# Moving one row tile's normalisation to GpSimd, and reordering the first norm, in a fused transformer block

## The chip, the cores and the metric

The kernel runs on one core of one Trainium2 chip. The metric is the device time of one execution in microseconds (us); lower is better.

Engine names: PE is TensorE (matmuls; PEld is its weight load, which overlaps it), DVE is VectorE, ACT is ScalarE, POOL is GpSimd, SP issues most of the DMA loads. The granted clock is the share of PE's full clock that a run's record shows (1.0 is full).

## The reference, cut to what matters

```python
mod = (_silu(c) @ w_mod).reshape(c.shape[0], 6, 1, -1)
sa, ca, ga, sb, cb, gb = ...                  # six rows of 1024: shift, scale, gate; twice
h = _layernorm(x, axis=-1) * (1 + ca) + sa    # x: 2048 x 1024, bf16
x = x + ga * _A_ref(h, A_wqkv, A_wo)          # linear attention; begins with h @ wqkv
h = _layernorm(x, axis=-1) * (1 + cb) + sb
x = x + gb * _B_ref(h, ...)                   # gated feed-forward, F = 3584
```

Only the start matters here. The first 512 rows of `x` (row tiles 0 to 3, each 128 x 1024) must be normalised, transposed and scaled before the first real matmul (q, the first third of `wqkv`) can run. The scale `ca` and shift `sa` are themselves products of 1 MB pieces of `w_mod` with one vector, done on PE as one-column matmuls.

## The kernel before: the parts in question

Every operation goes through a helper that derives the semaphore waits from the memory it touches, so the order of the calls is each engine's program order. The loads, on one DMA queue, in this order:

```python
for st in range(4):
    P.dma("x0_%d" % st, XRES[:, st, :], xv[:, st, :])      # 4 row tiles, 256 KB each
ca_load(0)        # scale columns 0-511, 1 MB, contiguous runs of 1024 bytes
wq_load(0, 2)     # query weights, rows 0-1 of 8 (each "row" is 128 x 1024)
ca_load(1)        # scale columns 512-1023
wq_load(2, 2); wq_load(4, 2)
sa_load(1)        # shift columns 512-1023
wq_load(6); wq_load(7)
sa_load(0)        # shift columns 0-511
```

The first norm, cut. `s0_`, `s1_`, `s3_` are the two `bn_stats` and the `bn_aggr` of tiles 0, 1 and 3 on VectorE; ScalarE sums tile 2 (`act_stats(2)`). `ln1_rstd1` adds epsilon on VectorE and takes the reciprocal root on GpSimd. `ln1_xn` normalises on VectorE, `ln1_xn_act(1)` on ScalarE:

```python
def ln1_xn(st):
    P.dve("tensor_scalar", out=XRES[:, st, :], in0=XRES[:, st, :],
          scalar1=MV[:, st, 0:1], scalar2=RSTD[:, st:st + 1], op0=ALU.subtract, op1=ALU.mult)

warm(13, bank=3)                       # matmuls on a constant, to keep PE's clock up
s0_[0](); s0_[1](); s1_[0](); s0_[2](); ln1_rstd1(0)
s1_[1](); s1_[2](); ln1_rstd1(1)
ln1_xn(0); tile_transposes(0); warm(5, bank=3)
s3_[0](); ln1_xn_act(1); tile_transposes(1)
m2[1](); m2[0](); neg_rstd(2)          # mean, variance, reciprocal root of tile 2
s3_[1](); s3_[2](); ln1_rstd1(3)
ln1_xn(2); ln1_xn(3)
mod_sc(WCA, 8, range(2)); fin_ca(0, 2) # scale columns 0-255: 16 one-column matmuls
tile_transposes(2, 3)
h0_first(0, "dve"); h0_first(1, "dve") # scaled, transposed tiles: q's operands
```

`q_phase_chunk0` then runs 4 q matmuls, the 16 one-column matmuls of scale columns 256-511, 10 more q matmuls, and so on; shift columns 512-1023 and 0-511 come in near the end of q.

The same `tensor_scalar` runs on GpSimd in one other place, on 128x512 pieces ahead of the feed-forward:

```python
P.pool("tensor_scalar", out=H2T[:, dt, :], in0=H2T[:, dt, :], scalar1=MODCOL[:, 2, dt:dt + 1],
       scalar2=MODCOL[:, 3, dt:dt + 1], op0=ALU.mult, op1=ALU.add)
```

## Time and profile before

| | before |
|---|---|
| median of 3 runs (lowest, highest) | 831.13 us (830.97, 832.21) |
| span of the profiled run | 829.3 us |
| PE busy | 823.3 us, 99% |
| first q matmul | 12.29 us |

The head of the page of the kernel before, with the busy time of each engine:

```profile
span 829.3 us, 10017 instructions
PE 823.3 (99%) x4083; PEld 378.8 (46%) x4083; DVE 312.9 (38%) x666; ACT 196.3 (24%) x335; POOL 40.5 (5%) x58
```

The end of the first part of the chain of waits (start, length, what), followed back from the last instruction:

```profile
9.78 0.79 POOL rstd L176
10.57 0.03 issue
10.60 0.56 DVE xres L176
11.16 0.05 issue
11.20 1.01 PE ps L176 x15
12.21 0.08 issue
12.29 814.80 PE ps L176 x4016
```

From 12.29 us on the chain is PE alone. Whatever delays the first q matmul, or makes PE wait after it, goes to the end of the program one to one. Ahead of it lies a chain over GpSimd (reciprocal root), VectorE (normalising tile 3) and PE (transposes).

PE's timeline of before around that point (start, busy time, instruction; in brackets the idle time before it and what ended it):

```profile
9.42 0.62 PE L176 MATMUL ps<-ident,xres 128*128 128x128 bf16 x8 [0.49 <-ACT xres L176]
9.87 0.54 PE L176 MATMUL ps<-siluc,wca 128*128 128x1 bf16 x16
...
11.20 1.01 PE L176 MATMUL ps<-ident,xres 128*128 128x128 bf16 x15 [0.71 <-DVE xres L176]
12.29 1.02 PE L176 MATMUL ps<-ht,wqk 128*128 128x512 bf16 x4
13.15 0.54 PE L176 MATMUL ps<-siluc,wca 128*128 128x1 bf16 x16
13.56 2.32 PE L176 MATMUL ps<-ht,wqk 128*128 128x512 bf16 x10
```

PE idles for short pieces before 12.29, then runs through, and the second block of 16 one-column matmuls (13.15) takes its time inside the solid stretch. GpSimd does four reciprocal roots in this time and is otherwise idle; the first two are those of tiles 0 and 1:

```profile
5.84 0.57 POOL L176 TENSOR_TENSOR rstd<-ve,neghalf 128x1 f32<-128x1 f32 x1 [4.44 <-DVE ve L176]
6.80 0.80 POOL L176 TENSOR_TENSOR rstd<-ve,neghalf 128x1 f32<-128x1 f32 x1 [0.39 <-DVE ve L176]
```

The view of one tile (minimum, median and maximum duration in ns, first and last start in us) gives GpSimd's existing `tensor_scalar`:

```profile
L176 POOL TENSOR_SCALAR h2t<-h2t,modcol x32: 762/768/1180, 230.9 to 649.4; 128x512 bf16<-128x512 bf16 x32
```

### The profile page before, as it was taken

Reading aid. Unit: us, or ns where it says so; the run is one execution under the profiler, and the core shown is the slowest. Engines: PE = TensorE matmul, PEld = TensorE weight load, DVE = VectorE, ACT = ScalarE, POOL = GpSimd, SP = SyncE. Lnnn points to the kernel's source line nnn. Section 1 sums busy time; section 2 is a strip of 40 time slices with the busy share of each in tenths; the row PEclk is TensorE's granted clock in tenths of the full one; section 3 lists DMA queues with packets and bytes.
Section 4 is the critical chain, followed back from the end, with each engine's and each line's share of the span. In section 5 each row is a group of like instructions: output and inputs, shape, how many; then the busy total and the mean of one; then the engine's idle time right before and its main releaser. Section 6 shows DMA issues by size and latency. Waiting matters only on the chain.

```text
span 829.3 us, 10017 instructions
## 1 busy us (share of the span) xinstructions
PE 823.3 (99%) x4083; PEld 378.8 (46%) x4083; DVE 312.9 (38%) x666; ACT 196.3 (24%) x335; POOL 40.5 (5%) x58
## 2 busy tenths in 40 slices
PE   8999999999999999999999999999999999999998
PEld 4544444454444444444444444444444444444444
DVE  5797986756955521121221111122111211221111
ACT  3658641323232111111111111111110111111011
POOL 1010000000130000030000003000000300000000
DMA  9969655938297986700455571045557004553000
GB/s 320 284 152 229 150 162 172 197 107 304 57 256 226 262 256 184 194 25 13 123 152 153 152 188 34 13 124 154 152 153 193 27 13 124 151 154 91 0 26 26
DMA packets 199246, 119.29 MB, mean 144 GB/s; under 512 B 57880, under 2 KB 182944, under 8 KB 199200
## 3 DMA queue, kind: packets, MB, share of 16 engines
q1 hardware_dynamic: 199184, 118.65, 53.0%
q8 instruction: 32, 0.52, 0.3%
q14 instruction: 14, 0.11, 0.0%
q10 hardware_dynamic: 16, 0.00, 0.0%
HBM read 100.67 MB, written 4.33 MB: 127 GB/s over the span
## 4 chain that ended last, share of the span: by engine, by line
PE 98%; DMA 1%; DVE 0%; ACT 0%; SPq 0%; POOL 0%; issue 0%
PE ps L176 98%; DMA xres<-in_A_x_dram 1%; ACT ht L176 0%; DVE xres L176 0%; SPq L176 0%; POOL rstd L176 0%; DVE stats L176 0%; DVE mv L176 0%; DVE ve L176 0%
## 5 line engine op out<-in xcount | busy, mean ns | idle before, releaser
L176 PE MATMUL ps<-h2t,gug 128*128 128x512 bf16 x896 | 211.7, 379 | 0.0
L176 PE MATMUL ps<-h2t,guu 128*128 128x512 bf16 x896 | 211.7, 379 | 0.0
L176 DVE TENSOR_TENSOR at<-sg,ps 128x512 bf16<-128x512 bf16 x112 | 77.0, 687 | 282.8 <-PE ps L176 281.2
L176 ACT ACTIVATE sg<-ps 128x512 bf16<-128x512 f32 x112 | 66.9, 597 | 309.7 <-PE ps L176 309.7
L176 PEld LDWEIGHTS ps<-h2t,guu 128*128 128x128 bf16 x896 | 87.7, 98 | 105.7
L176 PEld LDWEIGHTS ps<-h2t,gug 128*128 128x128 bf16 x896 | 87.6, 98 | 105.5
L176 PE MATMUL ps<-wd_a,at 128*128 128x512 bf16 (+1 forms) x512 | 112.4, 377 | 0.0
L176 PE MATMUL ps<-ht,wqk 128*128 128x512 bf16 x512 | 111.8, 379 | 0.1
L176 PE MATMUL ps<-wd_b,at 128*128 128x512 bf16 (+1 forms) x384 | 85.0, 377 | 0.0
L176 PEld LDWEIGHTS ps<-wd_a,at 128*128 128x128 bf16 x512 | 50.1, 98 | 59.7
L176 DVE TENSOR_TENSOR ut<-att,gb_b 128x512 bf16<-128x512 bf16 (+1 forms) x32 | 14.1, 441 | 167.0 <-ACT att L176 167.0
L176 PEld LDWEIGHTS ps<-ht,wqk 128*128 128x128 bf16 x512 | 49.4, 98 | 58.7 <-issue 0.2
L176 ACT ACTIVATE att<-ps 128x512 bf16<-128x512 f32 (+1 forms) x32 | 17.4, 591 | 182.1 <-PE ps L176 182.1
L176 PEld LDWEIGHTS ps<-wd_b,at 128*128 128x128 bf16 x384 | 37.6, 98 | 44.7
L176 PE MATMUL ps<-pk,xres 128*128 128x512 bf16 x256 | 56.5, 379 | 0.0
L176 PE MATMUL ps<-mw,pqt 128*128 128x512 bf16 x256 | 56.3, 379 | 0.0
L176 POOL TENSOR_SCALAR h2t<-h2t,modcol 128x512 bf16<-128x512 bf16 x32 | 26.3, 836 | 383.4 <-DMA h2t<-xn 383.4
L176 ACT ACTIVATE e<-ps 128x512 bf16<-128x512 f32 x56 | 33.1, 603 | 31.8 <-PE ps L176 21.3
L176 PEld LDWEIGHTS ps<-mw,pqt 128*128 128x128 bf16 x256 | 24.8, 98 | 30.2 <-DVE xres L176 0.4
L176 PEld LDWEIGHTS ps<-pk,xres 128*128 128x128 bf16 x256 | 24.8, 98 | 30.0 <-issue 0.4
L176 ACT ACTIVATE junk<-xres 128x1024 bf16<-128x1024 bf16 x24 | 25.4, 1058 | 35.1 <-DVE xres L176 34.9
L176 DVE SCALAR_TENSOR_TENSOR xres<-ps,xres 128x512 bf16<-128x512 f32 x32 | 21.4, 688 | 12.3 <-PE ps L176 11.5
(106 smaller groups left out, 345.1 us busy)
## 6 DMA issues: line engine op xcount, KB each, us to landing
gug<-in_B_w_gate_dram SPq DMA_DIRECT2D x56, 512.0 KB, 3.9
guu<-in_B_w_up_dram SPq DMA_DIRECT2D x56, 512.0 KB, 5.2
xres<-in_A_x_dram SPq DMA_DIRECT2D x20, 256.0 KB, 8.0
rb<-recip_den SPq DMA_DIRECT2D x8, 512.0 KB, 11.5
stgx<-in_w_mod_dram SPq DMA_DIRECT2D x2, 2048.0 KB, 7.8
wd_a<-in_B_w_down_dram SPq DMA_DIRECT2D x4, 1024.0 KB, 8.0
out_dram<-xres SPq DMA_DIRECT2D x31, 128.0 KB, 1.7
xres<-in_A_x_dram SPq DMA_DIRECT2D x3, 1024.0 KB, 14.2
```

The source lines that it names most:

```text
L176: return getattr(e, method)(**kw)
```

## The change

The intent: GpSimd, idle here, takes over tile 0, so that VectorE ends its sums earlier; scale columns 0-255 come in a load of their own and so earlier; and the matmuls of scale columns 256-511 move from the q phase into the time in which PE waits for q's first operand. The diff, cut:

```diff
-        ca_load(0)
+        ca_load(0, 256)
+        ca_load(256, 512)
         wq_load(0, 2)
-        ca_load(1)
+        ca_load(512, 1024)
...
+        def act_var(st): ...            # the variance of tile 2 in one step; one copy less
+        def xn_sums(st): ...            # ln1_xn with the mean read from ScalarE's sums
+        def xn_pool(st):
+            P.pool("tensor_scalar", out=XRES[:, st, :], in0=XRES[:, st, :],
+                   scalar1=MV[:, st, 0:1], scalar2=RSTD[:, st:st + 1], op0=ALU.subtract, op1=ALU.mult)
...
         s0_[0]()
         s0_[1]()
-        s1_[0]()
         s0_[2]()
         ln1_rstd1(0)
+        s1_[0]()
         s1_[1]()
         s1_[2]()
+        xn_pool(0)
         ln1_rstd1(1)
-        ln1_xn(0)
+        s3_[0]()
         tile_transposes(0)
-        warm(5, bank=3)
-        s3_[0]()
+        warm(3, bank=3)
+        mod_sc(WCA, 8, range(2))
+        s3_[1]()
         ln1_xn_act(1)
-        tile_transposes(1)
...
+        act_var(2)
         s3_[2]()
         ln1_rstd1(3)
-        ln1_xn(2)
+        xn_sums(2)
+        fin_ca(0, 2)
+        warm(1, bank=3)
+        tile_transposes(2)
+        tile_transposes(1)
         ln1_xn(3)
-        mod_sc(WCA, 8, range(2))
-        fin_ca(0, 2)
-        tile_transposes(2, 3)
+        tile_transposes(3)
+        mod_sc(WCA, 8, range(2, 4))
...
-            for nt in range(4):         # q phase
-                q_part(nt, qb[nt], (0,))
-            mod_sc(WCA, 8, range(2, 4))
```

Cut from this diff: the q matmuls on operand rows 0 and 1 are also grouped anew (both rows of the first four output groups, then of the other three), and `act_stats(2)` moves behind the call of `warm(13)`.

More of the change, by code (lines that the diff above doesn't have):

```diff
@@ L399, in bass_adaLN_cond__linear_attn_block__swiglu_ffn__prompt_kernel, with ca_load @@
             P.dma("x0_%d" % st, XRES[:, st, :], xv[:, st, :])
-        def ca_load(p):
-            P.dma("wca%d" % p, WCA[:, :, 512 * p:512 * p + 512], wmv[:, :, D + 512 * p:D + 512 * p + 512])
+        def ca_load(c0, c1):
+            P.dma("wca%d" % c0, WCA[:, :, c0:c1], wmv[:, :, D + c0:D + c1])
         def sa_load(p):
@@ L594, in neg_rstd, with act_var, xn_sums @@
             P.pool("tensor_tensor", out=RSTD[:, st:st + 1], in0=VE[:, st:st + 1], in1=NEGHALF[:, 0:1], op=ALU.pow)
-        act_stats(2)
         s0_, s1_, s3_ = ln1_stats_ops(0), ln1_stats_ops(1), ln1_stats_ops(3)
-        m2 = act_mv_ops(2)
+        def act_var(st):
+            P.dve("scalar_tensor_tensor", out=MV[:, st, 1:2], in0=SUMX[:, st:st + 1], scalar=SUMX[:, st:st + 1],
+                  in1=SUMSQ[:, st:st + 1], op0=ALU.mult, op1=ALU.subtract)
+            neg_rstd(st)
+        def xn_sums(st):
+            P.dve("tensor_scalar", out=XRES[:, st, :], in0=XRES[:, st, :],
+                  scalar1=SUMX[:, st:st + 1], scalar2=RSTD[:, st:st + 1], op0=ALU.subtract, op1=ALU.mult)
+        def xn_pool(st):
+            P.pool("tensor_scalar", out=XRES[:, st, :], in0=XRES[:, st, :],
+                   scalar1=MV[:, st, 0:1], scalar2=RSTD[:, st:st + 1], op0=ALU.subtract, op1=ALU.mult)
         def tile_transposes(*js):
@@ L607, in bass_adaLN_cond__linear_attn_block__swiglu_ffn__prompt_kernel @@
         warm(13, bank=3)
+        act_stats(2)
         s0_[0]()
         s0_[1]()
-        s1_[0]()
         s0_[2]()
         ln1_rstd1(0)
+        s1_[0]()
         s1_[1]()
         s1_[2]()
+        xn_pool(0)
         ln1_rstd1(1)
-        ln1_xn(0)
+        s3_[0]()
         tile_transposes(0)
-        warm(5, bank=3)
-        s3_[0]()
+        warm(3, bank=3)
+        mod_sc(WCA, 8, range(2))
+        s3_[1]()
         ln1_xn_act(1)
-        tile_transposes(1)
-        warm(0, bank=3)
-        m2[1]()
-        m2[0]()
-        neg_rstd(2)
-        s3_[1]()
+        act_var(2)
         s3_[2]()
         ln1_rstd1(3)
-        ln1_xn(2)
+        xn_sums(2)
[3 more added lines that the diff above has]
+        tile_transposes(1)
         ln1_xn(3)
-        mod_sc(WCA, 8, range(2))
-        fin_ca(0, 2)
-        tile_transposes(2, 3)
+        tile_transposes(3)
+        mod_sc(WCA, 8, range(2, 4))
         h0_first(0, "dve")
@@ L740, in q_phase_chunk0 @@
                 h0_first(dt, "dve")
-            for nts, dts in (((4, 5), (0,)), (range(6), (1,)), ((6,), (0, 1))):
+            for nts, dts in ((range(4), (0,)), (range(4), (1,)), ((4, 5, 6), (0, 1))):
                 for nt in nts:
```

## The prediction

> **What bounds the kernel now.** PE: the page gives it 823.3 us busy of a span of 829.3. The chain of waits holds one PE piece of 814.8 us that starts at 12.29 us (first q matmul) and never waits again. Before it lies the first norm, up to normalising tile 3 (until 11.15) and transposes (until 12.21). The change can gain only (a) an earlier q start and (b) scale matmuls moved out of the solid stretch into the idle time ahead of it.
>
> **What it removes, adds and moves (timeline of before).**
> - Normalising tile 0 leaves VectorE (0.54 us) for GpSimd. There 128x512 took 0.76 us; I estimate 1.5 us for 128x1024. Tile 1's reciprocal root on GpSimd then ends near 8.2, not 7.6 us; ScalarE has tile 2's sums until 8.23 anyway: tile 1 ready near 9.8, not 9.4.
> - VectorE finishes tile 3's statistics before tile 2's sums arrive and drops a copy (0.15 us). I estimate tile 2 ready at 10.15, tile 3 at 10.9 (before: 10.16 and 11.15).
> - Only 8 transposes, not 16, stay behind tile 3; then 16 scale matmuls (0.42 us of issue, before at 13.15 to 13.56) run while VectorE fills the first q operand. I estimate q to start at 12.0 to 12.1. Gain on PE alone: 0.6 us.
> - The 1 MB load of scale columns 0-511 becomes two of 0.5 MB; contiguous runs fall from 1024 to 512 bytes. In the trace 1024-byte packets took 47 to 52 ns, at 350 to 375 GB/s in the first 30 us; 512-byte ones (gate and up weights) 29 to 34 ns, at 290 to 330 GB/s. For 1 MB that is an estimated 0.45 to 0.65 us more. The Trainium skill, "DMA: Bandwidth & Descriptors", section "Why small descriptors are slow (HBM only)", names a fixed cost per packet; these times agree in direction.
>
> **How much lies on the critical path.** The DMA queue is full from 2 to 32 us, so a delay at its head reaches every later load. Landing against first use by PE: shift columns 512-1023 land at 20.79, used 21.05; shift columns 0-511 land at 25.16, used 25.38. Slack: 0.26 and 0.22 us. (Query weights: over 1 us.) A PE 0.6 us earlier catches up with these loads, and they come 0.45 to 0.65 us later. I expect shift columns 512-1023 at 21.2 to 21.45, PE waiting there 0.6 to 1.0 us, and the second shift load just in time. Net: the gain is lost and PE is 0.2 to 0.4 us later from 26 us on. Solid PE carries this to the end.
>
> **Prediction: 831.4 us**, range 830.5 to 832.3. Faster by over 2%: 0.01; within 2%: 0.98; slower by over 2%: 0.01.
>
> **What the profile would show.** Right: first q matmul at 11.9 to 12.3 us; a new PE wait for the shift columns near 20.5 to 21.4 us; 512-byte packets before 12 us at 28 to 34 ns; shift loads landing 0.3 to 0.7 us later; everything after 32 us unchanged in length. Wrong: no PE wait near 21 us and the span 0.5 us shorter (512-byte packets cost nothing here); or q starting after 13 us (GpSimd's normalisation takes longer than estimated).
>
> **What would make it wrong.** GpSimd taking over 2.5 us for tile 0, blocked by VectorE: the Trainium skill, "SBUF — State Buffer", section "SBUF: two separate sides", calls their shared port pair an exclusive lock; no run here shows it yet. Run-to-run spread (before: 830.97 to 832.21) exceeds the effect.

## The result, and the profile after

| | before | after |
|---|---|---|
| median of 6 runs (lowest, highest) | 831.17 us (830.83, 832.21) | 833.47 us (833.03, 833.79) |
| ratio of after to before | | 1.0026, 95% interval 1.0013 to 1.0039 |
| first q weight load | 12.26 us | 14.94 us |

Ratios here are the mean time of one kernel's fast runs over that of the other's in the same rounds, so they are not quite the ratio of the medians. At 2% the change is "same", as forecast. But it is slower by about 2.2 us, and 833.47 lies outside the stated range of 830.5 to 832.3.

GpSimd's timeline of the changed kernel:

```profile
5.35 0.56 POOL L176 TENSOR_TENSOR rstd<-ve,neghalf 128x1 f32<-128x1 f32 x1 [3.94 <-DVE ve L176]
6.01 3.79 POOL L176 TENSOR_SCALAR xres<-xres,mv,rstd 128x1024 bf16<-128x1024 bf16 x1
9.77 0.58 POOL L176 TENSOR_TENSOR rstd<-ve,neghalf 128x1 f32<-128x1 f32 x1
10.99 1.17 POOL L176 TENSOR_TENSOR rstd<-ve,neghalf 128x1 f32<-128x1 f32 x2 [0.64 <-DVE ve L176]
```

The instruction predicted at 1.5 us took 3.79. The reciprocal root of tile 1 has to queue behind it and ends at 10.35 us, not at 7.60 as before. VectorE takes its instructions in the order of the program here: the aggregation of tile 3's sums, which were complete at 8.33 us, came only at 10.83. So it stands still until that root is there, and with it the roots and normalisations of tiles 2 and 3:

```profile
7.04 1.29 DVE L176 BATCH_NORM_STATS2 stats<-xres 128x6 f32<-128x512 bf16 x2 [0.22 <-DMA xres<-in_A_x_dram]
10.38 0.21 DVE L176 TENSOR_SCALAR nmr<-mv,rstd 128x1 f32<-128x1 f32 x1 [2.06 <-POOL rstd L176]
10.83 0.20 DVE L176 BATCH_NORM_AGGREGATE mv<-stats 128x2 f32<-128x12 f32 x1
11.57 0.55 DVE L176 TENSOR_SCALAR xres<-xres,sumx,rstd 128x1024 bf16<-128x1024 bf16 x1 [0.36 <-POOL rstd L176]
12.52 0.54 DVE L176 TENSOR_SCALAR xres<-xres,mv,rstd 128x1024 bf16<-128x1024 bf16 x1
```

PE's timeline of the changed kernel:

```profile
9.86 0.86 PE L176 MATMUL ps<-ident,xres 128*128 128x128 bf16 x8 [2.28 <-POOL xres L176]
10.52 1.49 PE L176 MATMUL ps<-e,ident 128*128 128x512 bf16 x3
11.79 0.61 PE L176 MATMUL ps<-siluc,wca 128*128 128x1 bf16 x16
12.27 0.59 PE L176 MATMUL ps<-e,ident 128*128 128x512 bf16 x1
12.65 1.91 PE L176 MATMUL ps<-ident,xres 128*128 128x128 bf16 x24
14.40 0.54 PE L176 MATMUL ps<-siluc,wca 128*128 128x1 bf16 x16
```

PE waits 2.28 us for GpSimd's tile 0, and the second block of one-column matmuls now runs ahead of q, as intended. The chain of waits goes from GpSimd's tile 0 straight to PE, since the transposes of tile 0 stand first in PE's order:

```profile
6.01 3.80 POOL xres L176
9.81 0.05 issue
9.86 5.08 PE ps L176 x68
14.94 0.25 issue
```

So in this profile the result of the slow instruction is itself what PE waits for; the late roots lie beside the chain. From 9.86 us on PE has work without a wait up to q. One thing more is off: three warm-up matmuls took 1.49 us, where before five took 1.24. The view by stretches shows why (its first two columns are the stretch and its length, then the busy time of each engine, and the granted PE clock third from the end):

```profile
6.67:10.08 3.41, 1.13 (x8) 0.42 (x7) 1.43 (x3) 1.89 (x4) 3.41 (x2) 1.00 1.13 326
10.08:13.50 3.42, 3.42 (x36) 2.32 (x34) 1.93 (x8) 1.24 (x1) 1.43 (x3) 0.50 1.08 362
13.50:16.90 3.40, 3.15 (x42) 2.26 (x42) 2.42 (x6) 2.28 (x2) 0.00 (x0) 1.00 1.06 375
```

After a stretch in which PE worked 1.13 of 3.41 us, PE was granted half its clock for the next 3.41 us. The Trainium skill, "TensorE: Matmul & The Clock Gate", section "What's actually happening", describes it: a free-running window of 3413 ns, and half clock after an idle one. This trace agrees with the 3.41 us, though this window was 33% busy and not fully idle. Of the six timed runs four show it (granted clock 0.998 in the mean); these took 833.41 to 833.79 us, the two at full clock 833.03 and 833.27.

The account of the profiled run: the first q weight load is 2.68 us later (14.94 minus 12.26). (Weight loads are compared because one q matmul near the start is missing from the changed kernel's trace: 13 matmuls stand against 14 weight loads.) The weight load 3,800 from the end, which is past the shift work in both, is 2.28 us later (30.55 minus 28.27). The difference, 0.40 us, is about the 0.42 us of the moved block of one-column matmuls. So that part of the plan worked. The span grew by 2.4 us.

### The profile page after: what moved, and what is told of

Its sections match the earlier page's. It is cut to its first block, busy times and chain, and to the rows that moved or that the text cites. A ratio compares the mean times of both kernels' runs of the same rounds, so it can differ in the third digit from the quotient of the medians.

```text
span 831.7 us, 9937 instructions
## 1 busy us (share of the span) xinstructions
PE 820.3 (99%) x4004; PEld 379.9 (46%) x4082; DVE 312.2 (38%) x664; ACT 196.4 (24%) x335; POOL 44.2 (5%) x59
## 4 chain that ended last, share of the span: by engine, by line
PE 96%; DVE 2%; issue 1%; POOL 1%; DMA 0%; ACT 0%; DVEq 0%; ACTq 0%; POOLq 0%
PE ps L176 96%; DVE acc L176 1%; POOL xres L176 0%; DMA xres<-in_A_x_dram 0%; DVE pkt L176 0%; DVE stats L176 0%; DVE e L176 0%; DVE pqt L176 0%; DVE ht L176 0%; ACT e L176 0%; POOL rstd L176 0%; DVE xres L176 0%; DVE mv L176 0%; DVE modcol L176 0%; DVE ve L176 0%
```

## The experiments

All outputs are right. "Before" was run again in the same rounds each time.

### Why 3.79 us: three theories

*Operation*: GpSimd is slow at subtract-then-multiply. *Contention*: VectorE holds it up; VectorE's last sum ended at 8.33 us, and GpSimd ended 1.47 us later, at 9.80: just what a start at 8.33 and the estimated 1.5 us would give. *Size*: 1024 columns are slow.

**e0_probe**: the kernel before, with a ladder of GpSimd instructions on unused memory where GpSimd is idle, each form twice.

```diff
+ for _ in range(2):
+     probe(1024, ALU.mult, ALU.add, ml, ad)
+     probe(512, ALU.subtract, ALU.mult, me, rs)
+     probe(1024, ALU.subtract, ALU.mult, me, rs)
+     probe(512, ALU.mult, ALU.add, ml, ad)
+     ...  # 256 columns; in place; add-multiply; multiply-add with rs, me; multiply-subtract
```

> The kernel before, with a ladder of GpSimd tensor_scalar instructions on unused memory in the first chunk's down projection, where GpSimd is idle; each form twice: multiply-add and subtract-multiply at 256, 512 and 1024 columns, in place and not, plus add-multiply and multiply-subtract at 1024. Theory operation: multiply-add 1024 takes about 1.5 us and subtract-multiply 1024 about 3.8, 512 about 1.9. Theory size: both forms take 3.8 at 1024 and 0.76 at 512. Theory contention: both forms take 1.5 at 1024 where VectorE is quiet. The time of the kernel stays at 831.2 us, since GpSimd is idle there.

The time was 830.98 us (one run). GpSimd's timeline of this run; `mean,rstd` is subtract-multiply and `modcol` multiply-add, except the line at 375.89 (add-multiply) and the one at 378.48 (multiply-subtract):

```profile
361.36 1.20 POOL L176 TENSOR_SCALAR prb<-junk,modcol 128x1024 bf16<-128x1024 bf16 x1
362.66 2.08 POOL L176 TENSOR_SCALAR prb<-junk,mean,rstd 128x512 bf16<-128x512 bf16 x1
364.84 3.78 POOL L176 TENSOR_SCALAR prb<-junk,mean,rstd 128x1024 bf16<-128x1024 bf16 x1
370.00 1.26 POOL L176 TENSOR_SCALAR prb<-junk,mean,rstd 128x256 bf16<-128x256 bf16 x1
375.24 0.55 POOL L176 TENSOR_SCALAR prb<-junk,modcol 128x256 bf16<-128x256 bf16 x1
375.89 1.19 POOL L176 TENSOR_SCALAR prb<-junk,mean,rstd 128x1024 bf16<-128x1024 bf16 x1
378.48 3.79 POOL L176 TENSOR_SCALAR prb<-junk,rstd,mean 128x1024 bf16<-128x1024 bf16 x1
391.01 0.77 POOL L176 TENSOR_SCALAR prb<-junk,modcol 128x512 bf16<-128x512 bf16 x1
```

It is the operation, and within the pair it is the subtraction. Why GpSimd takes longer for it, no run here shows. Add-multiply and multiply-add take 1.19 to 1.20 us at 1024 columns; subtract-multiply and multiply-subtract take 3.78 and 3.79. From 512 to 1024 columns the slow form adds 1.70 us (3.3 ns a column), the fast one 0.43 us (0.84 ns). In place or not made no difference in the first pass (3.78 and 3.78); in the second the one in place took 3.96 us, beside VectorE `tensor_tensor` instructions. The expectation was off in one number: multiply-add at 1024 took 1.2 us, not the 1.5 that doubling gives. The Trainium skill, "GPSIMD Engine Reference", section 3.1, has 769 ns measured for 512 elements in its best case, which matches the 0.77 here; it says nothing of the subtraction. Contention exists too, but elsewhere: in the first pass multiply-add at 512 columns took 1.18 us, while VectorE ran `tensor_tensor` instructions with two SBUF inputs beside it.

**e3_quiet**: the changed kernel with VectorE kept silent while GpSimd works. Slower on purpose.

```diff
-        s1_[0]()
-        s1_[1]()
-        s1_[2]()
         xn_pool(0)
+        P.dve("tensor_copy", out=MODTMP[:, 15:16], in_=XRES[:, 0, 0:1])   # waits for GpSimd
+        s1_[0]()
+        s1_[1]()
+        s1_[2]()
```

> VectorE is kept silent while GpSimd normalises tile 0: a one-column copy on VectorE waits for GpSimd's result before tiles 1 and 3 are summed. Slower on purpose. Theory contention: GpSimd takes about 1.5 us (from 6.0 to 7.5 us). Theories operation and size: it takes 3.7 to 3.8 us as before, from 6.0 to 9.8 us.

VectorE and GpSimd in this run (836.28 us, one run):

```profile
6.21 3.78 POOL L176 TENSOR_SCALAR xres<-xres,mv,rstd 128x1024 bf16<-128x1024 bf16 x1
...
10.03 0.16 DVE L176 COPY modtmp<-xres 128x1 bf16<-128x1 bf16 x1 [4.64 <-POOL xres L176]
```

VectorE was idle for 4.64 us, over the whole of GpSimd's instruction, and it still took 3.78 us. Contention falls; the 9.80 us was a coincidence. This also agrees with the Trainium skill, "SBUF — State Buffer", section "Who interferes with whom", which says that a VectorE instruction with at most one SBUF input outside the two-port modes does not contend with GpSimd. `bn_stats` has one input here; whether it runs in a two-port mode, no run shows, but with it beside GpSimd the instruction took 3.79 us, and without it 3.78.

**e2_muladd**: the changed kernel with the same arithmetic on GpSimd in the fast form; the column minus-mean times rstd is made by VectorE in 0.16 us.

```diff
+        def xn_pool_ma(st):
+            P.dve("tensor_scalar", out=NMR[:, st:st + 1], in0=MV[:, st, 0:1], scalar1=RSTD[:, st:st + 1],
+                  scalar2=-1.0, op0=ALU.mult, op1=ALU.mult)
+            P.pool("tensor_scalar", out=XRES[:, st, :], in0=XRES[:, st, :],
+                   scalar1=RSTD[:, st:st + 1], scalar2=NMR[:, st:st + 1], op0=ALU.mult, op1=ALU.add)
-        xn_pool(0)
+        xn_pool_ma(0)
```

> GpSimd still normalises tile 0, but as multiply then add (x times rstd plus minus-mean-times-rstd) instead of subtract then multiply; VectorE makes the extra column. Theory operation: GpSimd is slow at this pair of operations, so it takes about 1.5 us (twice the 0.76 us of its 128x512 multiply-add), tile 0 is ready near 8.2 us instead of 9.8 and the time falls by 1 us or more. Theory contention (GpSimd is held up while VectorE works on its sums) and theory size (1024 columns are slow): it still takes 3 to 4 us, and the time stays at 833.5 us or above.

GpSimd's timeline of this run:

```profile
6.88 1.19 POOL L176 TENSOR_SCALAR xres<-xres,rstd,nmr 128x1024 bf16<-128x1024 bf16 x1 [0.98 <-DVE ve L176]
8.04 0.56 POOL L176 TENSOR_TENSOR rstd<-ve,neghalf 128x1 f32<-128x1 f32 x1
```

1.19 us instead of 3.79. The first q weight load went from 14.94 to 12.34 us. The median is 831.02 us against 830.87 of before in the same rounds, ratio 0.9999 (0.9985 to 1.0012). Changing the form of one instruction (and adding the column for it) takes the whole loss away.

### The other parts of the change

**e1_dve0**: tile 0 back on VectorE, the rest as changed (`xn_pool(0)` becomes `ln1_xn(0)`).

> Undoes one part of the change: tile 0 is normalised by VectorE again, at the same place in the order; loads and everything else as changed. If GpSimd's 3.79 us on tile 0 is what cost the time, q starts near 12.1 us (changed kernel: 14.9). Then two theories part. If that was the only loss, PE is 0.4 to 0.6 us ahead of the kernel before and the time is about 830.6 us. If the later landing of the loads also matters (in the changed kernel shift columns 512-1023 landed at 22.06 us instead of 20.79), PE now waits for them near 20.4 us for 0.7 to 1.6 us and the time is 831.5 to 832.2 us. If GpSimd was not the cause, the time stays at 833.5 us.

The median is 831.58 us (830.63 to 831.92) against 830.87; ratio 1.0002 (0.9989 to 1.0014). The first q weight load was at 12.52 us (I had expected 12.1). PE's weight loads show one new wait in the q phase, on query weights and not on the shift columns:

```profile
16.64 4.43 PEld L176 LDWEIGHTS ps<-ht,wqk 128*128 128x128 bf16 x22 [0.22 <-DMA wqk<-in_A_wqkv_dram]
```

The wait of 0.7 to 1.6 us for the shift columns that the second theory expected did not come. The wait shown costs PE 0.27 us: from the start of the 32 one-column matmuls to the next q matmul it is 1.07 us here (15.57 to 16.64) and 0.80 in the kernel before (15.71 to 16.51).

**e11_pool_only**: the kernel before, with tile 0 on GpSimd by subtract and multiply, and nothing else (`ln1_xn(0)` becomes the same instruction on GpSimd ahead of `ln1_rstd1(1)`).

> The kernel before with one part of the change alone: GpSimd normalises tile 0 by subtract and multiply, nothing else moves. Theory: the instruction takes 3.8 us, tile 1's reciprocal root behind it on GpSimd ends near 10.4 us instead of 7.6, everything behind is pushed by 2.2 to 2.9 us, and so is the end: 2.2 to 2.9 us over the kernel before. If the new order of the changed kernel was a part of the loss, this one loses clearly less than the changed kernel's 2.3 us.

834.0 us against 831.14, 2.9 us in the medians; ratio 1.0033 (1.0020 to 1.0045). GpSimd took 3.79 us here too. All five runs have a granted clock of 0.998. This one part alone loses more than the whole change: its profile ends 0.8 us later than that of the changed kernel (832.5 against 831.7). There, q starts 0.46 us later (weight load 15.41 against 14.94), and the 0.40 us of moved matmuls are not given back.

**e7_after_oneload**: the changed kernel with only the split of the load undone (`ca_load(0, 512)` again).

> Undoes the other part of the change alone: scale columns 0-511 in one load again, GpSimd still normalises tile 0 by subtract and multiply. Theory: with GpSimd at 3.8 us PE reaches every load so late (rows 2-3 of the query weights at 18.8 us against a landing near 16) that the loads cost nothing, so the time stays at that of the changed kernel, 2.0 to 2.5 us over the kernel before. Rival (the split of the load is a part of the loss even so): 0.4 us or more below the changed kernel's 2.3 us.

833.42 us against 831.14, 2.3 us in the medians, as the changed kernel had; ratio 1.0021 (1.0007 to 1.0034). As long as GpSimd makes PE late, the split costs nothing measurable.

**e6_split**: the kernel before, with only the split of the load.

```diff
-        ca_load(0)
+        ca_load(0, 256)
+        ca_load(256, 512)
```

> The kernel before with only the load of scale columns 0-511 split in two; no other change. Theory small packets: every later load lands 0.5 to 1.0 us later (rows 2-3 of the query weights near 16.3 us, first used at 16.49; shift columns 512-1023 at 21.2 or later, first used at 21.05), so PE meets a new wait in the q phase and the time rises by 0.2 to 0.6 us, to 831.1 to 831.5 us. Theory that the split costs nothing: landings and time as before, 830.9 us. Either way it is far too little for the 2.3 us that the whole change lost.

831.77 us against 831.34; ratio 1.0013 (1.0000 to 1.0026). This includes the profiled run of 835.51 us, which waited 2.6 us near 146 us for something else and had a half-clock window there (see below); without it the five others have a median of 831.73 us, and the ratio of the means is 1.0006. All six runs lie above the median of before, so a loss of some tenths is likely but not proven. PE's weight loads of that profile, where the kernel before has no wait on a load:

```profile
21.25 0.57 PEld L176 LDWEIGHTS ps<-siluc,wsa 128*128 128x128 bf16 x16 [0.21 <-DMA wsa<-in_w_mod_dram]
...
25.62 0.92 PEld L176 LDWEIGHTS ps<-siluc,wsa 128*128 128x128 bf16 x32 [0.26 <-DMA wsa<-in_w_mod_dram]
```

They wait for the two shift loads, as the prediction reasoned, but hardly: without a wait the kernel before has 0.12 and 0.13 us between the same weight loads. No matmul was held up. Those behind the two waits start 0.10 us later than in the kernel before (21.36 against 21.26, 25.69 against 25.59), and q had already started 0.10 us later (weight load 12.37 against 12.26). So this profile does not show what the split costs in time. The times at which loads had fully landed, read from the DMA completion events of all 14 profiles (us; mean, and range):

| load | one load of 1 MB (8 profiles) | split in two (6 profiles) |
|---|---|---|
| row tile 3 | 6.72 (6.20 to 7.41) | 7.09 (6.95 to 7.34) |
| scale columns 0-511, all | 10.02 (9.56 to 10.80) | 10.60 (10.43 to 10.88) |
| query rows 2-3 | 15.73 (15.28 to 16.51) | 16.34 (16.17 to 16.60) |
| shift columns 512-1023 | 20.53 (20.02 to 20.82) | 21.13 (20.65 to 22.06) |
| shift columns 0-511 | 25.01 (24.39 to 25.19) | 25.64 (25.22 to 26.52) |

With the split, everything behind it lands 0.6 us later on average, with a spread of the same size. It bought scale columns 0-255 at 8.7 to 9.1 us. Of the 0.6 us, 0.4 are already in row tile 3, which was issued ahead of the scale load; why, these runs do not settle.

### The clock, and better versions

**e9_warm**: the changed kernel with `warm(24)` for `warm(13)`, to fill PE's idle time.

> The changed kernel with 24 instead of 13 warm-up matmuls ahead of the first transposes, so that PE does not sit idle from 7.6 to 9.9 us. Four of the six timed runs of the changed kernel have a record of half the granted PE clock for 3.4 us starting at about 10.1 us, two have not and are 0.4 us shorter. Theory idle: PE's idle time brings the half clock; with warm-up matmuls all runs are granted full clock and the median falls from 833.5 to about 833.1 us. Rival: the half clock comes by chance; the share of runs with a clock of 0.998 stays near two in three and the time at 833.5 us.

All five runs had full clock, which fits the theory that PE's idle time brought the half clock. But the time did not fall: 833.73 us (832.66 to 834.03) against 831.34. In the profile the warm-up matmuls lasted until 10.63 us and held back the first transposes, so this run is no clean measure of the clock alone. Still, at full clock PE came from those transposes to the first q weight load in 3.6 us (14.23) instead of 5.08, and was 0.7 us ahead of the changed kernel at the weight load 3,600 from the end (73.00 against 73.72 us), and lost it again in a wait of about 1 us near 148 us. That wait (for a row that goes through device memory, ahead of the attention's G matmuls) was absent in the profile of before, 1.0 us here, 2.6 us in that of e6_split. It lies over 100 us behind the changed part, and may be a source of single runs 1 us or more above the rest; neither was tested.

**e5_oneload**: e2_muladd with the whole load again.

> The multiply-add kernel with scale columns 0-511 in one load of 1 MB again (runs of 1024 bytes). In the multiply-add kernel PE now waits about 0.2 us near 16.2 us for query weight rows 2-3, which landed at 16.32 us (15.34 in the kernel before). Theory small packets: with the whole load they land near 15.5 us again, this wait is gone, PE reaches the shift columns 0.2 to 0.3 us before the kernel before does and then waits for them; time 830.5 to 830.8 us. Rival: landing differs from run to run whatever the packets; then rows 2-3 land after 16 us here too and the time stays at 831.0 us.

831.37 us against 831.34; ratio 0.9999 (0.9986 to 1.0012). Query rows 2-3 landed at 15.83 us (expected: near 15.5), and PE no longer waited for them. But PE now waited for the scale columns, and the time did not fall:

```profile
10.15 0.55 PE L176 MATMUL ps<-siluc,wca 128*128 128x1 bf16 x16 [0.60 <-DMA wca<-in_w_mod_dram]
```

**e8_best**: e5_oneload, with GpSimd started earlier, tile 1's transposes ahead of tile 2's, and the uses of the two shift loads a little later in PE's order. (The recorded text says 2 groups for each; in the kernel each is one group later, of two matmuls and of one.)

> A try at a version that beats both: multiply-add on GpSimd, its extra column computed before tile 1's second half is summed (so GpSimd starts near 6.1 us), transposes of tile 1 ahead of tile 2, the whole 1 MB load, and the uses of the two shift loads moved 2 and 2 matmul groups later in PE's order. I expect q to start near 11.9 to 12.1 us, no PE wait on query weights, at most 0.2 us of wait on shift columns, and 830.3 to 830.6 us, 0.3 to 0.6 us below the kernel before. If the loads bind harder than read, it stays at 830.9 us.

831.10 us (830.44 to 831.84) against 831.34; ratio 0.9996 (0.9984 to 1.0008). In the profile the scale load landed at 10.80 us and PE waited 1.80 us for it.

**e10_best2**: as e8_best, with the matmuls of scale columns 0-255 moved behind the transposes of tiles 1 and 2.

> Second try at a better version: as the first try, but the matmuls of scale columns 0-255 behind the transposes of tiles 1 and 2, so that PE does not wait for the 1 MB load (in the profile of the first try it landed at 10.80 us and PE waited 1.8 us for it). I expect q to start near 12.2 to 12.4 us in every run, no wait for the scale load, small waits for query rows 2-3 or shift columns, and 0.2 to 0.5 us below the kernel before in median. If landing times that differ by half a microsecond from run to run decide, the interval of the ratio will hold 1.

830.70 us against 831.14; ratio 0.9995 (0.9983 to 1.0008).

**e12_best2_again**: the same kernel once more.

> The second try once more, unchanged, since its interval held 1 although four of its five runs lay at 830.6 to 830.7 us. In its profile PE was 0.43 us ahead of the kernel before at every mark after 23 us. If that is real, the median is again 0.3 to 0.5 us below the kernel before of the same rounds; if it was luck with the loads, the medians are within 0.2 us of each other.

831.02 us against 831.13; ratio 0.9999 (0.9986 to 1.0013). So there is no proven gain: what is left is decided by landing times that vary by half a microsecond.

## Why the prediction was wrong

- **What bounds the kernel: right.** The solid PE stretch carried the late q start to the end: 2.28 us late at 30.55 us, 2.4 us in the span. That the change would be "same" at 2% was right too, but with some 2 us of 831 at stake it shows nothing about the reasoning.
- **The step that failed is the cost of the added instruction**: "There 128x512 took 0.76 us; I estimate 1.5 us for 128x1024." It measured 3.79 us. The record it came from was multiply-then-add, and the added instruction subtracts. e0_probe shows the subtraction to cost about four times as much per column; e3_quiet excludes contention; e2_muladd and e11_pool_only show that this instruction alone makes the loss. The doubling was wrong as well, in the other direction: the fast form takes 1.19 us at 1024 columns.
- **What followed from it** was mis-sized in turn: tile 1's root at 10.35 us, not 8.2; tile 3 normalised at 13.06, not 10.9; q at 14.9, not 12.0 to 12.1. The sign that the prediction itself gave for this, q starting after 13 us, is what came. Even with the fast form (e2_muladd) q starts at 12.34 us. The estimate let 8 transposes of tile 3 come last; in the profile PE waits for tile 2, ready at 10.38 (estimated: 10.15), and is busy from 10.44 with 24 transposes and 16 one-column matmuls, 1.89 us in all.
- **The danger was named, with the wrong mechanism.** The prediction allowed for over 2.5 us "blocked by VectorE". In e3_quiet VectorE stood idle and the instruction took 3.78 us all the same.
- **The moved matmuls: right.** Predicted 0.42 us, measured 0.40.
- **The split of the load: the size fits, the wait did not come.** Predicted 0.45 to 0.65 us later, measured 0.6 on average; but 0.4 of it already stood in row tile 3, ahead of the split load, so the agreement does not confirm the reckoning and may be luck. In the changed kernel PE was so late that it waited for no load (shift columns 512-1023 landed at 22.06 us; their first weight load was at 23.33), so the forecast PE wait of 0.6 to 1.0 us near 21 us did not appear. In e6_split two weight loads waited there, without holding up a matmul. With GpSimd repaired it was query rows 2-3 that came short (e1_dve0), which the prediction had called safe.
- **Not foreseen**: half clock for 3.41 us, in four of six runs. The runs tie it to PE's idle time (none in the five of e9_warm), and the rule behind it stays open. Between the changed kernel's runs at full clock and those with such a window lie about 0.4 us (means 833.15 and 833.59); in e7_after_oneload it is 0.9 (832.59 and 833.50).

## What to carry to other kernels

Cost an instruction from a record with the same engine *and the same operations*; scaling a record of the same instruction with other operations was wrong by a factor of 2.5 here. For shapes like these, write a normalisation on GpSimd as multiply-add (or add-multiply) with a precomputed negative column, and not with a subtraction. And before moving work to an idle engine, look at who waits for its result and at what queues behind it there: here PE's first transposes waited for tile 0 itself, and the 0.6 us reciprocal roots of the other tiles stood behind its 3.8 us.

## What the Trainium skill lacked or had wrong

- "GPSIMD Engine Reference" (section 3.1 and the table of 4.1, which calls one-input operations roughly line-rate): it lacks that a subtraction in `tensor_scalar` is slow: 3.78 us for 128x1024 bf16 as subtract-multiply or multiply-subtract, against 1.19 us as multiply-add or add-multiply.
- "DMA: Bandwidth & Descriptors" (the specification table, which gives 512 bytes or more as the minimum for line rate): from 7.1 to 10.4 us, with the queue full, 329 GB/s were moved in the changed kernel (mostly runs of 512 bytes) and 376 in the kernel before (mostly of 1024 bytes). With 1 MB split into 512-byte runs later loads landed 0.6 us later on average, of which 0.4 were already in the load ahead of it.
- "TensorE: Matmul & The Clock Gate" (table of the two states): half clock is said to follow an idle window; here it followed a window that was 33% busy, and lasted one window of 3.41 us. In four more profiles it followed windows that were busy for 0.95 to 1.59 of 3.41 us (28 to 46%: e11_pool_only, e6_split, e7_after_oneload, e3_quiet).
